# Attention behind a sorted key order, then a token mixer: longer load packets, V sorted straight onto key partitions, X turned by transposing transfers

## The chip, the cores and the metric

One core of one Trainium2 chip runs the whole program. The metric is the device time of one execution in microseconds (us): the median over runs for a kernel, the span of one profiled execution for everything that is read from the profile. Engines are named as in the profile: PE is TensorE (matmuls), PEld its weight loads, DVE VectorE, ACT ScalarE, POOL GpSimd, SP the sync engine, which here only issues transfers. Transfers (DMA) run on 16 DMA engines whoever issues them.

## The reference

q, k and v have shape 4 x 8 x 768 x 64 (batch, head, token, feature), float32. The tokens of a head form 8 blocks of 96. A small matrix P per head, made of `sort_net` by five rounds of a Sinkhorn normalization, mixes the blocks of k and v; attention then runs inside each block; its output x (4 x 768 x 512) goes through a mixer over tokens.

```python
for _ in range(5):
    P = exp(P - max(P, -1)); P = P / sum(P, -1); P = P / sum(P, -2)
k_sorted = einsum('bhij,bhjcd->bhicd', P, k_blocks)
v_sorted = einsum('bhij,bhjcd->bhicd', P, v_blocks)
attn = softmax(q_blocks @ k_sorted^T / 8)          # inside each block of 96
x = (attn @ v_sorted) as (batch, token, 512)
wq, wk = x @ w_q, x @ w_k                           # 512 -> 64
mixed = (wq @ wk^T / 8) @ x
out = relu(mixed) @ w_out
```

## The kernel before

Everything is bf16 in SBUF, with float32 sums in PSUM. The work is cut into some 30 kinds of units, each named by a letter, the batch b and a running number n: `K21` is unit 1 of the K sort of batch 2. A capital letter is TensorE work that fills one or two of the eight PSUM banks; the small letter is the copy or the arithmetic that empties them, on ACT (A) or DVE (D). All units stand in one list, `ORDER`, written out as a table; every engine runs its own units in the order of that list, and semaphores hold it to the data. Nothing is reordered at run time, so a unit that waits holds everything behind it on its engine.

For one batch the stages are:

- `l` loads q, k and v, float32 to bf16 on the way, from the POOL queue; 128 partitions hold 128 groups of 6 neighbouring tokens of a head, so that a packet is 6 x 64 elements. The first q is loaded in float32 by two transfers of the sync queue and cast by `z`.
- `a`, `c`: the Sinkhorn rounds, exponentials on ACT and sums on DVE, once for all 32 heads. `B`, `u`, `n` spread the result into the sorting matrices M (`n`: one product with a mask, 512 elements per partition and half a batch).
- `Q`/`q`: q is turned so that features lie on partitions (QT). `K`/`k`: k is sorted and turned by one matmul with M (KT); the copy also brings the tokens back into block order.
- V. In batch 0, `Y`/`y` sort it like k, and `F`/`f` turn the result back so that keys lie on partitions (VT). In batches 1 to 3, `V`/`v` multiply with M as the weight and V as the moving side (three units of 8 matmuls, 128 columns each); the result Vs still has groups of tokens on partitions, and `R`, six transfers SBUF to SBUF per batch from the sync queue, moves it onto key partitions (VT).
- `S` scores (two heads side by side in the rows of the array), `e` exponential, `P` attention weights times V with a column of ones for the sums, `r` reciprocal, `x` product into X (96 keys x 512 features per block).
- `T`/`t` turn X on TensorE (batches 0 to 2), `D` turns it by two transposing transfers of the sync queue (batch 3), into XT. `J`/`j` multiply with w_q and w_k, `d` copies the q half to other partitions, `W`/`w` turn the k half, `G`/`g` and `H`/`h` are the mixer, `O`/`o` the output product with w_out, `s` the store.
- `U`/`z` turn the weights w_q and w_k into place, since they are loaded in long rows too. `Z` are matmuls on zeros that keep TensorE busy during the Sinkhorn rounds.

After the last unit a guard reduces the reciprocals on POOL and would take a slow general path for extreme numbers; it isn't taken here.

Of the kernel before, what the change touches and what calls it, by code (L numbers as in the profile page):

```python
# [8 lines left out]
FP32 = mybir.dt.float32  # L9
# [8 lines left out]
ORDER = """
i00:G i02:D lk0 c00:D lv0 A00:5 a01:A c01:D Z09:4 a02:A:5 z10:A c02:D Q00:7 a03:A c03:D z11:G i03:G
a04:A Q01:5 Z06:6 z13:A c04:D a05:A c05:D z12:G Q03:1 Q02:0 q03:D:1 q01:A:5 B00:3 n00:D:3 K00:4  # L20
n03:D:3 q00:A:7 K03:6 u00:A:3 q02:A:0 k00:A:4 n01:D:3 n02:D:3 k03:D:6 K01:0 Y02:2 k01:A:0 lv1 K02:4
lk1 y02:A:2 n11:G Y03:6 k02:D:4 y03:A:6 Y01:0 n10:G Y00:2 S06:4 F03:6 F02:7 y00:D:2 f03:D:6 f02:D:7
e06:A:4 S01:4 y01:A:0 e01:A:4 S00:2 F01:0 F00:1 S02:4 f01:D:0 V11:6 lq1 e00:A:2 V12:2 e02:A:4
f00:D:1 v11:D:6 v12:A:2 P00:0 n20:G V10:4 S03:6 v10:A:4 P01:2 r00:D:0 x00:D:0 e03:A:6 K13:0 k13:A:0
r01:D:2 x01:D:2 lp K11:4 k11:D:4 S05:6 K12:2 K10:0 e05:A:6 S04:4 k12:D:2 R10:S T00:6 e04:A:4 Q13:7
Q11:2 t00:D:6 k10:A:0 q13:D:7 R12:S Q10:3 R11:S P02:4 q11:D:2 r02:D:4 S16:0 S12:6 q10:A:3 P03:2
R13:S e16:A:0 U00:0 x02:D:4 r03:D:2 S11:4 lq2 x03:D:2 lk2 n30:G e12:A:6 S15:6 R14:S Q12:1 R15:S
z01:A:0 n21:G q12:D:1 T01:0 t01:D:0 P04:2 e11:A:4 T02:5 r04:D:2 x04:D:2 U01:4 S14:0 lv2 e15:A:6
z02:D:4 e14:A:0 n31:G S10:6 S13:2 T03:4 t03:D:4 lq3 Q20:0 e13:A:2 Q21:1 t02:D:5 q20:D:0 P12:2 lk3
q21:D:1 r12:D:2 e10:A:6 Q22:4 Q23:0 P11:6 x12:D:2 J01:1 r11:D:6 J00:5 q22:A:4 K23:2 x11:D:6 j01:D:1  # L30
q23:A:0 K21:6 j00:A:5 k23:A:2 K22:4 K20:0 k21:D:6 S25:2 k22:A:4 P14:6 W00:4 e25:A:2 T11:5 k20:D:0
W01:4 r14:D:6 t11:A:5 S26:2 e26:A:2 P13:0 x14:D:6 d00:S r13:D:0 w00:A:4 V21:6 V20:2 V22:4 x13:D:0
v20:D:2 T12:1 t12:D:1 d01:S T13:0 v21:A:6 v22:A:4 P10:6 S24:2 S22:4 lv3 G00:1 t13:D:0 r10:D:6 G01:1
e24:A:2 S21:2 x10:D:6 e22:A:4 Q33:0 Q30:6 g00:D:1 e21:A:2 T10:1 q33:D:0 q30:D:6 R21:S S20:4 H02:2
H01:6 t10:D:1 R25:S Q31:0 J10:1 R22:S h02:A:2 q31:D:0 H00:2 Q32:0 h01:D:6 e20:A:4 h00:D:2 S23:4
j10:A:1 J11:1 K33:6 R20:S K30:2 q32:D:0 e23:A:4 K31:4 R24:S j11:A:1 K32:0 k33:A:6 k30:D:2 k32:D:0
k31:A:4 R23:S S35:6 e35:A:6 S30:2 S32:4 S36:6 P21:0 r21:D:0 e30:A:2 P23:2 e36:A:6 e32:A:4 x21:D:0
r23:D:2 V31:6 V30:0 lo v31:A:6 v30:A:0 V32:4 v32:A:4 W11:7 x23:D:2 P22:2 R34:S W10:7 O02:6 P24:0
r22:D:2 x22:D:2 w10:A:7 R33:S P20:4 T22:7 o02:A:6 t22:A:7 r24:D:0 d11:S T21:3 t21:A:3 r20:D:4 R30:S
x24:D:0 O01:6 x20:D:4 T23:7 S34:0 S33:4 S31:2 R31:S e33:A:4 t23:D:7 G10:7 d10:S G11:7 e34:A:0  # L40
o01:A:6 e31:A:2 T20:4 g10:D:7 O00:5 H10:0 H11:6 t20:D:4 h10:D:0 R32:S h11:A:6 J21:4 o00:D:5 J20:2
j21:A:4 R35:S j20:A:2 P30:6 W21:3 P31:4 W20:3 s00:S r30:D:6 x30:D:6 P32:0 O03:2 r31:D:4 w20:A:3
P34:6 O05:3 x31:D:4 d21:S r32:D:0 o03:A:2 x32:D:0 r34:D:6 o05:A:3 P33:4 d20:S G20:2 G21:2 x34:D:6
H12:6 D30:S g20:A:2 h12:A:6 r33:D:4 O10:0 x33:D:4 H20:4 H22:2 H21:6 o10:D:0 O11:1 O12:0 D31:S
h21:D:6 h20:A:4 o11:A:1 o12:D:0 O04:6 o04:D:6 O13:1 O22:0 J31:7 j31:D:7 h22:A:2 J30:2 s10:S O14:3
s01:S W31:7 o13:A:1 o22:A:0 j30:A:2 w31:A:7 W30:6 O23:1 w30:A:6 d30:D o23:A:1 o14:D:3 s11:S d31:D
G30:0 s02:S G31:0 O15:7 g30:A:0 H31:4 H32:2 H30:0 h31:D:4 O20:6 o15:A:7 O21:7 O25:4 o21:D:7 o20:A:6
h32:A:2 O24:5 s12:S O34:3 O315:6 h30:A:0 s21:S o24:A:5 O314:0 O35:1 o25:D:4 o315:A:6 o314:A:0
o34:D:3 s20:S O32:6 s22:S O31:5 s314:A s34:A O33:7 o32:A:6 o35:D:1 O30:6 s315:A s35:S o33:A:7
o30:A:6 s32:S o31:D:5 s31:S s30:A s33:S  # L50
# [4 lines left out]
def kernel(  # L55
# [63 lines left out]
    XT = tiles("XT", 2, [P, PT, S])  # L119
# [28 lines left out]

# [24 lines left out]
    def u_a(b, n, e, bank):  # L173
        nc.scalar.activation(Pv, Pv, ACT.Exp)  # L174
# [18 lines left out]


# [6 lines left out]
    def u_i(b, n, e, bank):  # L201
# [274 lines left out]

    def guard():
# [213 lines left out]
```

## Time and profile before

| | us |
|---|---|
| median of 3 runs | 106.07 (105.77 to 108.18) |
| profiled execution: span from its first to its last instruction | 103.3 |
| mean granted TensorE clock, share of full speed | 0.983 |

The profile gives no other time of its own for that execution; the median of the runs lies 2.8 us over its span. In the rows shown below, a group row names the line, the engine, the operation and its tiles (output <- inputs) with partitions x elements, then count, busy time, mean duration in ns, and the idle time before. A timeline row begins with start and time in us, then engine, line, operation, tiles, and `xN` for N instructions in a row. In the page's slices one digit stands for a fortieth of the span and gives tenths. All matmuls share one line of code, L156, and all copies two (L160 on ACT, L164 on DVE), so tiles tell them apart.

### The profile page before, as it was taken

The page shows a single profiled execution, that of the slowest core. Times are in us where ns is not written, and L with a number is a line of the kernel's source. Part 1 is how long each engine was busy: PE and PEld are TensorE (multiplying, and loading weights), DVE is VectorE, ACT ScalarE, POOL GpSimd, SP SyncE. Part 2 cuts the span into 40 slices and gives each one's busy share as a digit, 9 for nine tenths or more (in the row PEclk, how much of TensorE's full clock was granted, in tenths as well). Part 3 has the DMA queues.
Part 4 walks back from the last instruction along what each step waited for, and adds up shares of the span by engine and source line. Part 5 has one row for each costly group of instructions (what it writes and reads, how often), then busy time and mean ns, then how long its engine had stood idle before and what let it go on. Part 6 is the DMA issues. An engine that isn't in the chain of part 4 may idle for free.

```text
span 103.3 us, 3449 instructions
## 1 busy us (share of the span) xinstructions
PE 86.1 (83%) x1461; PEld 61.6 (60%) x1467; DVE 70.7 (68%) x137; ACT 71.1 (69%) x103; POOL 26.2 (25%) x43
## 2 busy tenths in 40 slices
PE   4947259998996969989899668999998999999950
PEld 2234159897784756978667457785874445546510
DVE  2677784799986797969879747957899733355210
ACT  4263667799899555897868889879646574558440
POOL 7376348690499700000000000000005700000000
PEclk9999995999999999999999999999999999999999
DMA  1799999999999999999999900264335799168993
GB/s 25 283 334 213 203 203 206 203 204 206 199 239 249 230 204 204 205 208 216 199 236 246 213 14 0 69 173 116 141 106 129 175 400 382 43 247 362 347 348 117
DMA packets 22032, 20.91 MB, mean 202 GB/s; under 512 B 4097, under 2 KB 20353, under 8 KB 22017
## 3 DMA queue, kind: packets, MB, share of 16 engines
q0 software_dynamic: 12256, 9.31, 58.1%
q1 hardware_dynamic: 9184, 10.73, 31.4%
q10 hardware_dynamic: 576, 0.66, 1.7%
q8 instruction: 11, 0.18, 0.7%
q14 instruction: 5, 0.03, 0.1%
HBM read 20.19 MB, written 6.29 MB: 256 GB/s over the span
## 4 chain that ended last, share of the span: by engine, by line
PE 33%; DMA 22%; DVE 21%; issue 8%; ACT 8%; SPq 2%; POOL 2%; ACTq 0%; DVEq 0%
PE ps L156 33%; DMA Qn<-in_q_dram 11%; DMA VT<-Vs 8%; DVE X L384 8%; ACT E L355 4%; SPq L316 2%; DVE Rall L379 2%; DMA out_dram<-ot 2%; POOL M L254 2%; DVE KT L164 2%; ACT ot L160 2%; DMA Pm<-in_sort_net_dram 1%; DVE Pm L197 1%; DVE tmp L195 1%; ACT Pm L174 1%
## 5 line engine op out<-in xcount | busy, mean ns | idle before, releaser
L355 ACT ACTIVATE E<-ps 96x960 bf16<-96x960 f32 (+1 forms) x28 | 24.0, 899 | 4.1 <-PE ps L156 3.8
L156 PE MATMUL ps<-wo,mixT 128*128 128x512 bf16 (+1 forms) x98 | 21.6, 362 | 0.4 <-issue 0.2
L384 DVE TENSOR_TENSOR X<-ps,Rall 96x896 bf16<-96x896 f32 (+1 forms) x20 | 20.0, 1003 | 0.6
L156 PEld LDWEIGHTS <-mixT 128*128 128x128 bf16 x104 | 9.5, 98 | 8.9 <-issue 0.8
L160 ACT COPY ot<-ps 128x512 f32<-128x512 f32 (+2 forms) x17 | 9.5, 560 | 6.9 <-PE ps L156 6.6
L156 PE MATMUL ps<-VT,E 96*128 96x65 bf16 x256 | 11.0, 193 | 0.9 <-DMA VT<-Vs 0.7
L487 POOL CROSS_LANE_REDUCE s<-Rall 96x1 f32<-96x280 f32 x1 | 0.8, 756 | 42.8 <-DVE Rall L379 42.8
L156 PEld LDWEIGHTS <-E 96*128 96x128 bf16 x256 | 9.5, 97 | 2.6 <-DMA VT<-Vs 0.8
L156 PEld LDWEIGHTS <-KT 64*128 64x128 bf16 (+1 forms) x288 | 8.3, 97 | 4.1 <-issue 2.6
L156 PE MATMUL ps<-QT,KT 64*128 64x96 bf16 x256 | 8.9, 204 | 2.1 <-ACT E L355 1.0
L156 PE MATMUL ps<-idb,Qn 128*64 128x128 bf16 x192 | 7.5, 222 | 3.8 <-ACT Qn L160 2.2
L164 DVE COPY ot<-ps 128x512 f32<-128x512 f32 (+1 forms) x10 | 6.4, 637 | 5.9 <-PE ps L156 4.8
L164 DVE CAST KT<-ps 128x768 bf16<-128x768 f32 x9 | 8.4, 953 | 2.8 <-PE ps L156 2.5
L254 POOL TENSOR_TENSOR M<-PTR,m_p 128x512 bf16<-128x512 bf16 x6 | 7.8, 1304 | 8.4 <-PE ps L156 5.5
L156 PEld LDWEIGHTS <-Qn 128*64 128x64 bf16 x192 | 5.7, 109 | 6.0 <-ACT Qn L160 3.2
L447 ACT ACTIVATE mixT<-ps 128x1024 bf16<-128x1024 f32 x7 | 7.1, 1025 | 3.0 <-PE ps L156 3.0
L156 PE MATMUL ps<-M,Kn 128*64 128x128 bf16 x192 | 7.5, 231 | 1.9 <-ACT QT L160 0.6
L160 ACT CAST KT<-ps 128x768 bf16<-128x768 f32 x11 | 8.6, 801 | 0.7 <-PE ps L156 0.7
L156 PEld LDWEIGHTS <-Kn 128*64 128x64 bf16 x192 | 6.6, 116 | 2.8 <-issue 1.8
L379 DVE RECIPROCAL Rall<-ps 96x14 f32<-96x14 f32 (+1 forms) x20 | 4.6, 228 | 4.8 <-PE ps L156 4.5
L449 DVE TENSOR_SCALAR mixT<-ps 128x1024 bf16<-128x1024 f32 x5 | 6.0, 1221 | 2.4 <-PE ps L156 2.3
L160 ACT CAST Vs<-ps 128x1024 bf16<-128x1024 f32 x7 | 6.8, 1019 | 0.6 <-ACT E L355 0.4
(81 smaller groups left out, 130.8 us busy)
## 6 DMA issues: line engine op xcount, KB each, us to landing
out_dram<-ot SPq DMA_DIRECT2D x9, 512.0 KB, 3.5
Kn<-in_k_dram POOLq DMA_DIRECT2D x4, 768.0 KB, 15.4
Vn<-in_v_dram POOLq DMA_DIRECT2D x4, 768.0 KB, 13.1
VT<-Vs SPq DMA_DIRECT2D x18, 132.0 KB, 6.6
Qn<-in_q_dram POOLq DMA_DIRECT2D x3, 768.0 KB, 14.0
XT<-in_q_dram SPq DMA_DIRECT2D x2, 768.0 KB, 5.9
out_dram<-ot SPq DMA_DIRECT2D x3, 256.0 KB, 2.0
wo<-in_moe_w_out_dram POOLq DMA_DIRECT2D x1, 512.0 KB, 25.5
```

What stands on the lines that cost most here:

```text
L156: nc.tensor.matmul(o, w, x, is_transpose=t, start=start, stop=stop, skip_group_check=True)
L160: nc.scalar.copy(o, i)
L164: nc.vector.tensor_copy(o, i)
L174: nc.scalar.activation(Pv, Pv, ACT.Exp)
L195: nc.vector.reduce_sum(tmp, (Pm if n == 1 else Pv).rearrange("p i j -> p j i"), axis=AX.X)
L254: ENG[e].tensor_tensor(out=M[b % 2][:, h0:h0 + hn], in0=src.unsqueeze(2).to_broadcast([P, hn, SP, NB]), in1=m_p.unsqueeze(1).unsqueeze(3). ...
L316: ENG[e].dma_start(out=VT[b % 2].rearrange("(s r) i h x -> r s i (h x)", r=R6)[n], in_=Vs[0][:, n].rearrange("p h e -> p (h e)"))
L355: nc.scalar.activation(E[b % 2][:, n, 0:2 * w * BLK].rearrange("p (t a c) -> p a t c", a=2, c=BLK), PS[0:BLK, bank:bank + 2, 0:w * BLK].re ...
L379: nc.vector.reciprocal(Rall[:, b, n, :, 0:w], avps(bank, w)[:, :, :, D])
L384: nc.vector.tensor_mul(xo.rearrange("p (a t d) -> p a t d", a=2, d=D), avps(bank, w)[:, :, :, 0:D], Rall[:, b, n, :, 0:w].unsqueeze(3).to_ ...
L447: nc.scalar.activation(o, i, ACT.Relu)
L449: nc.vector.tensor_relu(o, i)
```

## The change

Six things change together, and `ORDER` is new throughout (it has 12 units of Q and of K instead of 16, and so on).

- Loads of q and k: a partition holds 24 neighbouring tokens of a head, and four heads make 128 partitions; a packet is 24 x 64 elements (3 KB in bf16). Q and K then take three units per batch of 16 matmuls, with two halves of heads in the columns of the array, and copies of 1024 columns. The first q comes in six transfers of the sync queue (three pieces of 8 tokens, two halves of heads), and ACT casts its three pieces.
- Load of V: a partition holds one block of 96 tokens (64 partitions for a batch, two batches in one tile), in packets of 8 KB read.
- V's sort: the units `V` (four per batch, 16 matmuls each, in all four batches) take for each feature d the column `Vn[..., d]`, 96 keys, as the weight, and a matrix MV of 64 columns as the moving side. The output has keys on partitions at once; `Y`, `F`, `Vs` and the transfers `R` go.
- X of batches 1, 2 and 3 is turned by transposing transfers (`D`); only batch 0 keeps `T`.
- The weights w_q, w_k are loaded straight into place; `U` goes. The masks Lk, Lv, m_k, m_v are made at the start, mostly on POOL; M is 256 elements per partition and batch.
- `W` turns both halves of qkT (8 matmuls of 128 columns), and the copy takes one half; `H` has twice the matmuls with half the columns; the last stores of batch 3 are of whole rows of 512.

```diff
 ORDER = """
-i00:G i02:D lk0 c00:D lv0 A00:5 a01:A c01:D Z09:4 a02:A:5 z10:A c02:D Q00:7 a03:A c03:D z11:G i03:G
...
+i00:G ls0:S i02:D lk0:G A00:0 ls1:S m00:A:0 lv0:G i04:G ls2:S c00:D a01:A c01:D lq1:G i03:G a02:A
+z00:A c02:D Q00:0 z01:A lk1:G Z08:1 q00:D:0 lv1:G a03:A z02:A c03:D lp:G lo:G a04:A c04:D Z06:0
...
 """
-    NIN = 3
-    Qn, Kn, Vn = (tiles(n, NIN, [P, H, R6, D]) for n in ("Qn", "Kn", "Vn"))
+    QT4 = P // NP // NB
+    CT = BLK // QT4
+    C8 = 8
+    NC = CT // C8
+    C4 = CT // R6
+    NV = 4
+    Qn = tiles("Qn", NQ, [P, 2, CT, D])
+    Kn = tiles("Kn", NK, [P, 2, CT, D])
+    Vn = tiles("Vn", 2, [P, BLK, D])
...
-    QT = tiles("QT", 2, [P, NP, R6, P])
-    KT = tiles("KT", 2, [P, NP, S + PAD])
-    Vs = tiles("Vs", 1, [P, R6, H, DV])
-    VT = tiles("VT", 2, [BLK, NB, H, DV])
+    QT = tiles("QT", 2, [P, CT, NP, NB * QT4])
+    KT = tiles("KT", 2, [P, NPR * BLK + PAD])
+    VT = tiles("VT", 2, [BLK, 2, H, NB, DV])
...
+        elif n[0] == "v":
             b = int(n[1])
-            nc.gpsimd.dma_start(out=t[b % NIN][:, h0:h1].rearrange("p h r d -> p h (r d)"),
-                                in_=src[b, h0:h1].rearrange("h (p r) d -> p h (r d)", p=P))
+            nc.gpsimd.dma_start(out=Vn[b // 2][half(b)].rearrange("p c d -> p (c d)"),
+                                in_=v[b].rearrange("h (j c) d -> (h j) (c d)", c=BLK),
+                                max_dma_last_dim=VDESC)
...
+        else:
+            t, src = {"q": (Qn, q), "k": (Kn, k)}[n[0]]
+            b = int(n[1])
+            nc.gpsimd.dma_start(out=t[b % len(t)].rearrange("p a c d -> p a (c d)"),
+                                in_=src[b].rearrange("(a h) (j c) d -> (h j) a (c d)", a=2, c=CT))
...
     def u_Q(b, n, bank):
-        for r in range(R6):
-            for hh in range(2):
-                mm(bf(bank)[hh * D:(hh + 1) * D, r * P:(r + 1) * P],
-                   Qn[b % NIN][:, 2 * n + hh, r, :], idb, t=True)
+        for c in range(C8):
+            for a in range(2):
+                mm(bf(bank)[a * D:(a + 1) * D, c * P:(c + 1) * P], Qn[b % NQ][:, a, n * C8 + c, :], idb, t=True)
...
     def u_K(b, n, bank):
-        sort_turn(Kn, b, n, bank)
+        ps = flat(bank)
+        for c in range(C8):
+            for a in range(2):
+                mm(ps[a * D:(a + 1) * D, c * P:(c + 1) * P], Kn[b % NK][:, a, n * C8 + c, :], M[:, b, a, :])
 
     def u_k(b, n, e, bank):
-        in_blocks(KT[b % 2], n, e, bank)
+        copy(e, KT[b % 2][:, 0:NPR * BLK].rearrange("p (u q n c) -> p n u q c", q=QT4, n=NC, c=C8)[:, n],
+             flat(bank).rearrange("p (c u q) -> p u q c", c=C8, q=QT4))
...
     def u_V(b, n, bank):
         ps = flat(bank)
-        for h in range(H):
-            mm(ps[:, h * P:(h + 1) * P], M[b % 2][:, h].rearrange("p s i -> p (s i)"),
-               Vn[b % NIN][:, h, 2 * n:2 * n + 2, :].rearrange("p r d -> p (r d)"))
+        for m in range(D // NV):
+            mm(ps[0:BLK, m * D:(m + 1) * D], Vn[b // 2][half(b), :, n * D // NV + m], MV[half(b), b // 2, :])
 
     def u_v(b, n, e, bank):
-        copy(e, Vs[0][:, 2 * n:2 * n + 2, :, 0:D].rearrange("p r h d -> p h r d"),
-             flat(bank).rearrange("p (h r d) -> p h r d", h=H, r=2))
-
-    def u_R(b, n, e, bank):
-        ENG[e].dma_start(out=VT[b % 2].rearrange("(s r) i h x -> r s i (h x)", r=R6)[n],
-                         in_=Vs[0][:, n].rearrange("p h e -> p (h e)"))
...
+        w = D // NV
+        copy(e, VT[b // 2][:, b % 2].rearrange("p h i x -> p (h i) x")[:, :, n * w:(n + 1) * w],
+             flat(bank)[0:BLK, :].rearrange("p (d u) -> p u d", d=w))
 
     def u_S(b, n, bank):
...
-                   KT[b % 2][o:o + D, kp, i * BLK:i * BLK + P],
-                   QT[b % 2][o:o + D, kp, :, i * SP:(i + 1) * SP])
+                   KT[b % 2][o:o + D, pr * BLK:pr * BLK + P],
+                   QT[b % 2][o:o + D, :, kp, i * QT4:(i + 1) * QT4].rearrange("p (c r) t -> p r c t", r=R6))
...
     def u_W(b, n, bank):
+        if n >= 10:
+            for i in range(NB):
+                mm(bf(bank)[0:BLK, i * P:(i + 1) * P], qkT[b % 2][:, i * BLK:(i + 1) * BLK], idb, t=True)
+            return
...
     def u_H(b, n, bank):
         for p2 in range(2):
-            for a in range(2):
-                qq = (qkT, qD)[a][b % 2][a * DH:(a + 1) * DH, :]
-                mm(PS[:, bank + a, p2 * 256:(p2 + 1) * 256],
-                   Ab[b % 2][a * DH:(a + 1) * DH, p2 * P:(p2 + 1) * P],
-                   qq.rearrange("p (i r s) -> p r i s", i=NB, r=R6)[:, 2 * n:2 * n + 2])
+            for r in range(2):
+                for a in range(2):
+                    qq = (qkT, qD)[a][b % 2][a * DH:(a + 1) * DH, :]
+                    mm(PS[:, bank + a, p2 * 256 + r * P:p2 * 256 + (r + 1) * P],
+                       Ab[b % 2][a * DH:(a + 1) * DH, p2 * P:(p2 + 1) * P],
+                       qq.rearrange("p (i r c t) -> p r i t c", i=NB, r=R6, c=C4)[:, 2 * n + r])
```

What the change moves on three engines is shown by the order of their instructions, before and after. On the sync queue, behind the load of q of batch 0 (VT the sorted V, Vs its form before the transfers, qD and qkT the mixer's q), there stood:

```order
L316 DMA VT_86<-Vs_84 16x8x528 x6
L411 DMA qD_95<-qkT_93 64x384 x2
L316 DMA VT_85<-Vs_84 16x8x528 x6
L316 DMA VT_86<-Vs_84 16x8x528 x2
L411 DMA qD_96<-qkT_94 64x384
```

Now there stands, at the same place (XT is X turned, ot the output's buffer):

```order
L397 DMA qD_90<-qkT_88 64x384 x2
L376 DMA_TRANSPOSE XT<-X_86 128x16x96 x2
L461 DMA out_dram<-ot_100 128x1024
L397 DMA qD_91<-qkT_89 64x384 x2
L376 DMA_TRANSPOSE XT<-X_85 128x16x96 x2
```

The transfers of sorted V are gone, and transposing transfers of X stand between those of qD. On ACT, at the start of the program (Pm is the Sinkhorn matrix, Qn q of batch 0 in bf16), before:

```order
L174 ACTIVATE Pm<-Pm 32x64 x2
L176 CAST m_p<-ps 128x16
L160 CAST Qn_69<-XT_91 128x768
L174 ACTIVATE Pm<-Pm 32x64
L178 COPY Lx<-idb 32x512
```

and after:

```order
L182 ACTIVATE Pm<-Pm 32x64 x2
L168 CAST Qn_69<-XT 128x2x512 x2
L182 ACTIVATE Pm<-Pm 32x64
L168 CAST Qn_69<-XT 128x2x512
L182 ACTIVATE Pm<-Pm 32x64 x2
```

Two casts of q now stand ahead of the third exponential and one ahead of the fourth; POOL had a part of them before. On TensorE, in a unit of V's sort (M and MV the sorting matrices, Vn the loaded V), before:

```order
L156 LDWEIGHTS M_109
L156 MATMUL ps<-Vn_77,M_109 128x128
L156 LDWEIGHTS M_109
L156 MATMUL ps<-Vn_77,M_109 128x128
L156 LDWEIGHTS M_109
```

and after:

```order
L164 LDWEIGHTS Vn_74
L164 MATMUL ps<-MV,Vn_74 96x64
L164 LDWEIGHTS Vn_74
L164 MATMUL ps<-MV,Vn_74 96x64
L164 LDWEIGHTS Vn_74
```

V has moved from the moving side to the weights.

More of the change, by code (lines that the diff above doesn't have):

```diff
@@ L23 @@
[L23 to L40, printed above, removed]
@@ L449, in u_h @@
             nc.vector.tensor_relu(o, i)
[L451 to L454 removed]
     def u_O(b, n, bank):
[L457 removed]
         for t in range(PT):
[L459 to L460 removed]
+            mm(PS[:, bank, :], mixT[b % 2][:, t // 2, t % 2, n, :], wo[:, t, :], start=(t == 0), stop=(t == PT - 1))
     def oslot(b, n):
```

219 lines of the change are left out of this document (110 added, 109 removed).

## The prediction, made blind

> **What bounds the kernel now.** I read the page's header, slices and chain first, then the timeline of TensorE and the groups by shape.
>
> ```profile
> span 103.3 us, 3449 instructions
> PE 86.1 (83%) x1461; PEld 61.6 (60%) x1467; DVE 70.7 (68%) x137; ACT 71.1 (69%) x103; POOL 26.2 (25%) x43
> PE   4947259998996969989899668999998999999950
> GB/s 25 283 334 213 203 203 206 203 204 206 199 239 249 230 204 204 205 208 216 199 236 246 213 14 0 69 173 116 141 106 129 175 400 382 43 247 362 347 348 117
> q0 software_dynamic: 12256, 9.31, 58.1%
> HBM read 20.19 MB, written 6.29 MB: 256 GB/s over the span
> PE ps L156 33%; DMA Qn<-in_q_dram 11%; DMA VT<-Vs 8%; DVE X L384 8%; ACT E L355 4%; SPq L316 2%; DVE Rall L379 2%; DMA out_dram<-ot 2%; POOL M L254 2%; DVE KT L164 2%; ACT ot L160 2%; DMA Pm<-in_sort_net_dram 1%; DVE Pm L197 1%; DVE tmp L195 1%; ACT Pm L174 1%
> ```
>
> The busy shares of 68 to 83% name no bound, so I cut the program at the first sorting matmul of V of batch 3. These timeline rows of TensorE (start, time, operation) give the cut, its two ends and the rates I use; the rate is (time of the row minus one matmul's own latency) over (count minus one).
>
> ```profile
> 13.42 0.86 PE L156 MATMUL ps<-M,Kn 128*64 128x128 bf16 x24 [0.52 <-DVE M L254]
> 19.97 0.60 PE L156 MATMUL ps<-QT,KT 64*128 64x96 bf16 x20
> 20.50 1.09 PE L156 MATMUL ps<-idb,KT 128*96 128x128 bf16 x16
> 41.31 1.53 PE L156 MATMUL ps<-M,Kn 128*64 128x128 bf16 x48
> 44.94 0.61 PE L156 MATMUL ps<-VT,E 96*128 96x65 bf16 x14
> 45.39 1.50 PE L156 MATMUL ps<-Vn,M 128*128 128x128 bf16 x24
> 47.01 0.84 PE L156 MATMUL ps<-idb,X 96*128 96x96 bf16 x16
> 61.07 0.61 PE L156 MATMUL ps<-Vn,M 128*128 128x128 bf16 x8
> 68.45 1.06 PE L156 MATMUL ps<-X,wk 96*64 96x256 bf16 x16
> 71.30 1.47 PE L156 MATMUL ps<-XT,wqk 128*128 128x384 bf16 x8
> 80.17 4.49 PE L156 MATMUL ps<-wo,mixT 128*128 128x512 bf16 x20
> 86.66 0.51 PE L156 MATMUL ps<-idb,qkT 128*96 128x64 bf16 x8
> 90.69 8.83 PE L156 MATMUL ps<-wo,mixT 128*128 128x512 bf16 x47
> ```
>
> ```profile
> L156 PE MATMUL ps<-Vn,M x72: 216/219/229, 21.8 to 63.1; 128*128 128x128 bf16 x72
> ```
>
> With that latency of 0.2 us (0.3 to 0.4 for the rows of 384 and 512 columns) this makes 28 ns for a matmul of K or a turn of q, some 20 for a score, 32 for E times V, 56 for V's sort, 58 for a turn of sorted V, 42 for a turn of X, 43 for a turn of wk, 52 for G, 163 for XT, 216 for the output. The order puts into stage A (13.4 to 61.1, 47.7 us) 240 matmuls of K and of V's f32 sort and 144 turns of q (10.8 us), 226 scores (4.5), 156 of E times V (5.0), 48 sorts and 32 turns of V (4.6), 64 turns of X (2.7), 16 XT (2.6) and small ones (2.3): 32.4 us, 68%. Stage B (61.1 to 99.5, 38.4 us) holds the equal of 96 output matmuls (20.7), 100 of E times V (3.2), 16 XT (2.6), 48 G (2.5) and 6.3 of the rest: 35.3 us, 92%. So stage B is bound by TensorE, and stage A by something else: loads, copies and VT's transfer, which the chain names. Behind the last matmul come 3.8 us of copy and store up to 103.3, and 106.07 (the median) lies 2.8 us over the span of the profiled execution. I add 6.6 us to the end of TensorE's work.
>
> **The change part by part.** *Loads.* 203 to 206 GB/s stand in the load slices, and queue 0 counts written bf16 bytes (9.31 MB against 20.19 MB read), so the read rate is near 406 GB/s, as fast as the store slices at their best (400). Longer packets I cost at nothing: from no gain up to 2 us if 5% were left. VT's SBUF transfers go, 12 of them inside the load phase; the transposing transfers of batch 1 come in.
>
> ```profile
> VT<-Vs SPq DMA_DIRECT2D x18, 132.0 KB, 6.6
> XT<-X SPq DMA_TRANSPOSE x2, 3.7
> wo<-in_moe_w_out_dram POOLq DMA_DIRECT2D x1, 512.0 KB, 25.5
> 34.74 0.78 POOL L228 DMA_DIRECT2D wo<-in_moe_w_out_dram x1
> ```
>
> The last load lands at 34.7 + 25.5 = 60.2. Twelve transfers are 1.6 MB, 4 us at 400 GB/s and 8 at 203; I take 5. The two transposing ones cost 0 (hidden) to 7.4 (two landings); I take 2. The last load, now V of batch 3, then lands near 57. That is a floor for the cut, no gain by itself.
>
> On the sync queue the six VT transfers of a batch and their waits are replaced by two of X (the first pair of orders above). Nothing waits at E times V for a transfer any more; what waits for the transposing one is J, several units behind.
>
> *Copies.* The rows by shape:
>
> ```profile
> L160 ACT CAST KT<-ps 128x768 bf16<-128x768 f32 x11 | 8.6, 801 | 0.7 <-PE ps L156 0.7
> L164 DVE CAST KT<-ps 128x768 bf16<-128x768 f32 x9 | 8.4, 953 | 2.8 <-PE ps L156 2.5 <-ACT KT L160 0.2
> L160 ACT CAST Vs<-ps 128x1024 bf16<-128x1024 f32 x7 | 6.8, 1019 | 0.6 <-ACT E L355 0.4
> L164 DVE COPY QT<-ps 128x768 bf16<-128x768 bf16 x10 | 5.3, 548 | 1.9 <-PE ps L156 1.9
> L164 DVE COPY XT<-ps 128x768 bf16<-128x768 bf16 x9 | 4.8, 552 | 1.0 <-PE ps L156 0.7
> L164 DVE COPY VT<-ps 96x1024 bf16<-96x1024 bf16 x4 | 2.6, 680 | 0.2 <-PE ps L156 0.2
> L164 DVE CAST Vs<-ps 128x1024 bf16<-128x1024 f32 x2 | 2.4, 1217 | 0.0
> ```
>
> Twelve copies of turned X become 4; K goes from 16 of 768 to 12 of 1024 columns; V's 9 + 4 (Vs and the f32 sort of batch 0) + 4 (VT) become 16 of 1024; q's 16 become 12. At these durations (1024 columns of q by VT's 680 on DVE, 1.0 on ACT) DVE saves 4.9 us and ACT 3.3 in all. Because the order moves seven exponentials behind the cut, stage A itself loses 6.9 us of DVE and 5.2 of ACT. KT was read from PSUM with large steps already, so the stepped reads of the new copies cost nothing extra.
>
> *Start.* ACT now casts q in three pieces of 1024 columns (0.83 us x 1024/768 = 1.1) between the exponentials of the Sinkhorn chain (the second pair).
>
> ```profile
> 6.85 0.26 ACT L174 ACTIVATE Pm<-Pm 32x64 f32<-32x64 f32 x1
> 8.61 0.26 ACT L174 ACTIVATE Pm<-Pm 32x64 f32<-32x64 f32 x1 [1.00 <-DVE Pm L197]
> 8.79 0.83 ACT L160 CAST Qn<-XT 128x768 bf16<-128x768 f32 x1
> ```
>
> Pieces of q thus stand ahead of the exponentials that ran at 6.85 and 8.61, and the last q landed only for 8.79. Waiting for it and casting (8.8 + 1.1 = 9.9) puts the fourth exponential 1.3 us later; with a q copy that DVE now has inside the chain I take 1.5 (bounds 0.5 and 3). K starts at 14.9.
>
> *V's weights, the term that decides.* In the third pair of orders the data became the weight: 96 columns that lie 64 elements (128 bytes) apart, with 64 moving columns. There are 256 such pairs for 72 of 56 ns, 48 of 28 and 32 of 58 (7.2 us). The lower bound is the turn of wk, also 96 weight columns against 64 moving ones but side by side: 43 ns. No weight of this trace is read with steps. The nearest rows are a reduction on DVE over the same 32x64 tile, along rows (L190) and across them with 32-byte steps (L195):
>
> ```profile
> L190 DVE TENSOR_REDUCE tmp<-Pm x5: 207/207/207, 3.1 to 10.8; 32x8 f32<-32x64 f32 x5
> L195 DVE TENSOR_REDUCE tmp<-Pm x5: 253/255/269, 3.8 to 11.5; 32x8 f32<-32x64 f32 x4, 32x8 f32<-32x72 f32 x1
> ```
>
> Eight more stepped elements cost 14 ns, 1.75 ns each; KT and Vs casts of DVE give (1217 - 953)/256 = 1.03 ns for one more element elsewhere. Stepped reading is 1.7 times as slow. Taken as a ratio, a pair costs 43 x 1.7 = 73 ns; taken as a time, 96 x 1.75 = 168. I take 73, as an engine's own rate scales with it, and keep 43 and 168 as ends.
>
> [...]
>
> *TensorE's sum.* In stage A the order now holds 304 matmuls of K and turns of q (8.5 us), 178 scores (3.6), 142 of E times V (4.5), 32 turns of X (1.3), 12 XT (2.0), 12 output matmuls (2.6) and 2.0 of small ones: 24.5 us, and 192 of V's pairs. Stage B: 84 output matmuls (18.1), 114 of E times V (3.6), 20 XT (3.3), 48 G (2.5), 78 scores (1.6) and 4.3 of the rest: 33.4 us, and 64 pairs. At 73 ns that is 38.5 and 38.1 (before 32.4 and 35.3). For stage A's filling I take 80%, midway between 68% (copies and loads, which are relieved) and 92% (TensorE alone): 38.5/0.80 = 48.1. So the cut falls at 14.9 + 48.1 = 63.0, TensorE ends 38.1/0.92 = 41.4 later at 104.4, and with 6.6 the time is 111.0. Stage A at 92% is held by the loads to 57 and gives 105.0; at 68% it gives 119.5. H's matmuls of 128 columns in twice the number, and turns of wk with 128 columns, I cost at 0.4 us, within these.
>
> **The rivals.** *Steps cost the weights nothing* (43 ns). Stage A holds 32.7 us of TensorE work and is bound by copies: 47.7 - 5.2 (ACT, the smaller gain) = 42.5, cut at 57.4, just over the loads; stage B 36.2/0.92 = 39.3; 103.3 us. For it: 128 weight columns of E are loaded every 32 ns and 96 of wk's turn only every 43, so the path that reads weights has slack in one of them. Against: the reduction rows. Range 101 to 106.
>
> *A line costs a fixed time* (168 ns): TensorE binds both stages at 92%: 56.8/0.92 = 61.7, 44.2/0.92 = 48.0, 131.2 us. For it: 1.75 ns is the only direct reading. Against: it is a reading of another engine, which takes 1.03 ns for an element side by side where a weight column takes 43/96 = 0.45.
>
> *The transposing transfers come late.* They queue among the loads; if batch 1's land only when loads end (57 + 3.7), J and with it the cut in the fixed order stand at 61, as before, even with free weights: 61 + 39.3 + 6.6 = 106.9. For it speak VT's transfers, which took 6.6 us to land among the loads; against it J's distance of some ten units from the issue.
>
> **How the numbers follow.** Forecast 0.43, free steps 0.37, fixed line time 0.12, late transfers 0.08. A measurement of this kernel tells about 2% from no change: 103.9 to 108.2. Faster: four fifths of the free case, 0.30. Same: the rest of it, most of the late case and a quarter near the lower end of the forecast, 0.20. Slower: 0.50. The forecast's own range is 105 to 119.5; with the free case the range for 8 in 10 is 101 to 119.5, leaving out the fixed line time. The time is that of the likeliest, 111.0.
>
> **What would show it.** The spacing of the 16 matmuls in a unit of V: about 0.7 us a unit is the free case, 1.2 to 1.4 the forecast, 2.7 the fixed time. The fourth exponential near 9.9 and the first K near 14.9 show the start right. The first V unit of batch 3 near 63 with TensorE above 75% before it shows stage A; near 57 the free case. J of batch 1 waiting for a transfer shows the late case; the last load landing near 57 shows the loads' sum. The forecast is wrong if V's units run at 0.7 us and the cut falls before 60.

## The result: 152.1 us, where 111.0 was forecast

The changed kernel takes 152.14 us (median of 6 runs, 150.63 to 152.99) against 105.85 (104.51 to 108.18, 6 runs): a ratio of 1.4385 with a 95% interval of 1.4283 to 1.4488. The direction was forecast, the size was not: 152 lies far outside 101 to 119.5. Some runs of the experiments had a lower clock than others of the same kernel; ratios, and the times of e1, e3 and e9 below, leave them out.

The page of the changed kernel: header, slices of TensorE and its clock, first queue, chain by line, and the two costliest groups (busy us, mean ns of one, idle time before). Behind it stands the clock's slices of the kernel before.

```profile
span 148.8 us, 3565 instructions
PE 128.5 (86%) x1542; PEld 101.0 (68%) x1542; DVE 67.9 (46%) x121; ACT 70.2 (47%) x93; POOL 21.6 (15%) x52
PE   1392039999999999999899999999999999999980
PEclk9999555555589555557975599999975799999998
q0 software_dynamic: 4368, 9.31, 33.4%
PE ps L164 76%; DMA XT<-in_q_dram 9%; DVE X L370 1%; SPq L256 1%; ACT KT L168 1%; ACT E L341 1%; ACT Qn L168 1%; ACT QT L168 1%; ACT ot L168 0%; DVE tmp L202 0%; DVE Rall L365 0%; DVE Pm L201 0%; DVE tmp L199 0%; ACT Pm L182 0%; DVE tmp L203 0%
L164 PE MATMUL ps<-MV,Vn 64*96 64x64 bf16 x256 | 43.4, 339 | 0.0
L164 PEld LDWEIGHTS <-Vn 64*96 64x96 bf16 x256 | 42.6, 253 | 0.4 <-issue 0.2
```

```profile
PEclk9999995999999999999999999999999999999999
```

Three things differ from the page of before. The chain is three quarters TensorE, where it was one third; the costliest group is V's sort, 43.4 us busy where all of V's sort and turns came to 7.2 by the forecast's rates; and TensorE's slices are full or nearly so from the seventh to the last but one, although its clock stands at half speed in 15 of the 40 slices (mean 0.778, before 0.983). DVE and ACT have hardly less work (67.9 and 70.2 us, before 70.7 and 71.1) but wait for it: the view of waits puts 27.7 us of DVE's and 19.2 of ACT's idle time down to copies of V that wait for TensorE.

The timeline of TensorE shows the start (first two rows), a turn of X beside a unit of V, and the first unit of V of batch 3:

```profile
23.84 2.77 PE L164 MATMUL ps<-M,Kn 128*64 128x128 bf16 x48
26.54 9.69 PE L164 MATMUL ps<-MV,Vn 64*96 64x64 bf16 x58
54.81 2.10 PE L164 MATMUL ps<-idb,X 96*128 96x96 bf16 x24
56.84 2.82 PE L164 MATMUL ps<-MV,Vn 64*96 64x64 bf16 x16
95.60 2.77 PE L164 MATMUL ps<-MV,Vn 64*96 64x64 bf16 x16
```

The first K stands at 23.84, where 13.42 was before and 14.9 was forecast. A unit of V takes 2.6 us from start to start (16 pairs of 163 ns, the median distance of two starts). The X row gives (2.10 - 0.28)/23 = 79 ns a turn, by the reading of the forecast that made it 42 before: the granted clock is 0.50 from 54 to 57 us, where it was 1.00 at the turns of before (47.0 to 47.8). The cut of the forecast, the first unit of V of batch 3, is at 95.6 instead of 63.

ACT's timeline shows why K is late:

```profile
4.94 1.03 ACT L168 CAST Qn<-XT 128x1024 bf16<-128x1024 f32 x1
11.68 1.04 ACT L168 CAST Qn<-XT 128x1024 bf16<-128x1024 f32 x1 [5.71 <-DMA XT<-in_q_dram]
12.63 0.25 ACT L182 ACTIVATE Pm<-Pm 32x64 f32<-32x64 f32 x1
17.47 1.04 ACT L168 CAST Qn<-XT 128x1024 bf16<-128x1024 f32 x1 [4.59 <-DMA XT<-in_q_dram]
18.42 0.25 ACT L182 ACTIVATE Pm<-Pm 32x64 f32<-32x64 f32 x1
```

The second and the third piece of q land for 11.68 and 17.47, and the third and fourth exponential of the Sinkhorn chain, which stand behind their casts in ACT's row, run at 12.63 and 18.42 (before 6.85 and 8.61). So there are two suspects, the steps of V's weights and the late q, and a third that may only follow from them, the halved clock.

### The profile page after: what moved, and what is told of

It is laid out like the page before. It is cut to its first block, busy times and chain, and to the rows that moved or that the text cites. A ratio compares the mean times of both kernels' runs of the same rounds, so it can differ in the third digit from the quotient of the medians.

```text
span 148.8 us, 3565 instructions
## 1 busy us (share of the span) xinstructions
PE 128.5 (86%) x1542; PEld 101.0 (68%) x1542; DVE 67.9 (46%) x121; ACT 70.2 (47%) x93; POOL 21.6 (15%) x52
## 4 chain that ended last, share of the span: by engine, by line
PE 76%; DMA 9%; ACT 5%; DVE 4%; SPq 2%; issue 1%; ACTq 0%; DVEq 0%
PE ps L164 76%; DMA XT<-in_q_dram 9%; DVE X L370 1%; SPq L256 1%; ACT KT L168 1%; ACT E L341 1%; ACT Qn L168 1%; ACT QT L168 1%; ACT ot L168 0%; DVE tmp L202 0%; DVE Rall L365 0%; DVE Pm L201 0%; DVE tmp L199 0%; ACT Pm L182 0%; DVE tmp L203 0%
## 5 line engine op out<-in xcount | busy, mean ns | idle before, releaser
L164 PE MATMUL ps<-MV,Vn 64*96 64x64 bf16 x256 | 43.4, 339 | 0.0
L164 PEld LDWEIGHTS <-Vn 64*96 64x96 bf16 x256 | 42.6, 253 | 0.4 <-issue 0.2
L164 PE MATMUL ps<-wo,mixT 128*128 128x512 bf16 x96 | 24.7, 400 | 0.0
L172 DVE CAST VT<-ps 96x1024 bf16<-96x1024 f32 x9 | 11.0, 1221 | 27.7 <-PE ps L164 27.7
L168 ACT CAST VT<-ps 96x1024 bf16<-96x1024 f32 x7 | 7.1, 1015 | 19.2 <-PE ps L164 19.2
L168 ACT COPY ot<-ps 128x512 f32<-128x512 f32 x15 | 8.7, 587 | 8.1 <-PE ps L164 7.0
L164 PEld LDWEIGHTS <-KT 64*128 64x128 bf16 x256 | 9.8, 111 | 3.5 <-issue 2.4
L168 ACT CAST KT<-ps 128x1024 bf16<-128x1024 f32 x10 | 9.8, 1015 | 2.7 <-PE ps L164 2.6
L172 DVE COPY ot<-ps 128x512 f32<-128x512 f32 x9 | 6.2, 687 | 5.8 <-PE ps L164 5.7
L172 DVE COPY QT<-ps 128x1024 bf16<-128x1024 bf16 x9 | 6.2, 685 | 4.7 <-PE ps L164 4.6
```

Source lines behind the costliest of these rows:

```text
L164: nc.tensor.matmul(o, w, x, is_transpose=t, start=start, stop=stop, skip_group_check=True)
L168: nc.scalar.copy(o, i)
L172: nc.vector.tensor_copy(o, i)
```

## The experiments

They are called e1 to e10 in the order in which they were run. Times are medians, with a ratio to runs of the kernel before on the same chip where there were several rounds. e5, an earlier form of e10, gave no time. Of longer edits the lines that matter are shown; `...` marks what is left out.

**e1: the steps of the weights taken away.** In this kernel and the others with weights side by side, V's weights are read from the same tile in another order, so the output is of other data; the number of pairs, the matmul shapes and the loads stay.

```diff
+VSTEP = (1, 1, 1, 1)
...
-mm(ps[0:BLK, m * D:(m + 1) * D], Vn[b // 2][half(b), :, n * D // NV + m], MV[half(b), b // 2, :])
+st = VSTEP[b]
+w = Vn[b // 2][half(b)].rearrange("p c d -> p (c d)")
+o = (n * D // NV + m) * (BLK if st == 1 else 1)
+mm(ps[0:BLK, m * D:(m + 1) * D], w[:, o:o + (BLK - 1) * st + 1:st], MV[half(b), b // 2, :])
```

> The changed kernel, with V's weights read side by side (96 neighbouring elements of the same tile instead of one feature of 96 keys; V's sort and so the output are of other data, everything else is the same work). Theory S (a weight column that lies 128 bytes from its neighbour costs a fixed 1.7 ns, so a pair took 163 ns): the pairs come down to 43 to 46 ns, TensorE loses 256 x 0.119 = 30 us of work, mean granted clock back above 0.9, time 112 to 120, since the late start (K at 23.8 instead of 13.4) stays. Rival C (the halved clock is the cause and V its victim): pairs stay above 80 ns, clock stays below 0.85, time above 140.

Measured: 115.0 us, a ratio of 1.0833 (1.0723 to 1.0944). A row of its timeline and the groups of its waits at TensorE:

```profile
44.55 0.90 PE L165 MATMUL ps<-MV,Vn 64*96 64x64 bf16 x16
PE ps L165 <- ACT Qn L169: 12.6, 2, 8.4
```

A pair takes 45 ns. 256 x (163 - 45) = 30.2 us of the 37 us gained are the pairs themselves; the rest comes with a clock whose mean rises from 0.778 to 0.935, and this run doesn't take it apart. The steps are shown to be the main cause. Some 9 us over the kernel before are left, and the waits name the casts of q.

**e4 and e8: what a step costs.** Two kernels gave each batch another step in V's weights (output of other data but where the step is 64): the code of e1 with steps of 2, 4, 8 and 16 elements in the first, and of 1, 4, 2 and 64 in the second:

```diff
+VSTEP = (2, 4, 8, 16)
```

> The changed kernel with another step between V's weight columns in each batch: 2, 4, 8 and 16 elements (4, 8, 16, 32 bytes) for batches 0 to 3 (V's sort of other data). If the price goes by 16-byte lines at 1.7 ns each: 43 ns a pair at step 2 (4 columns a line), about 82 at step 4, 163 at 8 and at 16. [...] If any step costs the full price: 163 at all four.

> The weights of V in steps of 1, 4, 2 and 64 elements of 2 bytes for the batches 0, 1, 2 and 3 (output of other data for batches 0 to 2). In e4 the step of 2 elements fell into a stretch in which the granted clock was 0.50, where e3 shows 80 ns a pair for weights side by side too. Theory S (a load of weights takes a time for each 16 bytes touched by its reading, some 1.7 to 1.9 ns, so for 96 columns 24 x 1.8 = 43 ns with 2 elements' steps, which hides behind the pair's own 45): batch 1 near 91 ns a pair, batch 2 near 45 (80 where the clock is 0.50), batch 3 at 163. Rival (any step but 1 costs a price of its own, or the price goes with the clock): batch 2 at 80 with the clock at 1.00, or batch 1 and 3 other than 91 and 163. Time by S near 126: 116.7, 64 x 46 ns for batch 1 and 64 x 118 ns for batch 3 more, and a lower clock in batch 3.

Measured: 143.06 and 128.43 us, one run each. Units of V in the timelines, first two of the first kernel (steps of 8 and 16 elements), then three of the second (4, 2 and 64):

```profile
78.41 2.96 PE L165 MATMUL ps<-MV,Vn 64*96 64x64 bf16 x16
85.91 3.02 PE L165 MATMUL ps<-MV,Vn 64*96 64x64 bf16 x16
```

```profile
46.94 1.65 PE L165 MATMUL ps<-MV,Vn 64*96 64x64 bf16 x16
60.97 2.40 PE L165 MATMUL ps<-MV,Vn 64*96 64x64 bf16 x48
73.02 2.77 PE L165 MATMUL ps<-MV,Vn 64*96 64x64 bf16 x16
```

The median distances of two starts, with the clock granted in the unit's stretch (the row of 2 bytes from e1, e3 and e8, that of 128 bytes from the changed kernel and e8, the others from e4 and e8):

| step of the 96 columns | at clock 1.00 | at clock 0.50 |
|---|---|---|
| 2 bytes (side by side) | 45 ns | 80 ns |
| 4 bytes | 47 ns | 80 ns |
| 8 bytes | 91 ns | 91 ns |
| 16 bytes | 176 ns | 176 ns |
| 32 bytes | 180 ns | 180 ns |
| 128 bytes | 163 ns | 163 ns |

Up to 4 bytes the pair is as fast as side by side and goes with the clock. From 8 bytes on it doesn't go with the clock; at 1.00 it about doubles from 4 to 8 and from 8 to 16 bytes (47, 91, 176 ns) and grows no further (180, 163). So I count by the 16-byte pieces that the 96 columns touch (48 at 8 bytes, 96 from 16 bytes on): 91/48 to 163/96, 1.7 to 1.9 ns a piece everywhere; at 4 bytes the same count makes 24 x 1.85 = 44 ns, an estimate that lies within the 45 of a pair side by side. The expectation by this count (91, 45, 163) came out. Two columns in a piece (8 bytes' steps) cost 91 ns against 45 side by side, and four (4 bytes' steps) 47.

**e2, e3, e6 and e7: the late q.** The packets by start time, from the transfer records of the trace (number of packets in 1 us, mean ns of one):

```
          before: queue 0 | queue 1    after: queue 0 | queue 1
 4-5 us      0            252, 65         51, 249       67, 70
 5-6 us      0            276, 61         49, 250       50, 95
 6-7 us     81, 78        170, 70         48, 247       48, 96
 8-9 us    252, 78         23, 51         49, 254       49, 94
12-13 us   268, 79          0             39, 322       42, 96
```

Queue 0 carries GpSimd's loads, queue 1 the sync queue's q (16 of its 67 packets from 4 to 5 us are of 4 bytes only). Before, q had the transfers to itself up to 6 us, and 387 and 399 GB/s in the two rows from 4 us on. Now k0, issued at 1.52 us (before at 1.45), sends from 4.1 us on where it was 6.2, and the two queues are served packet by packet: 48 of one, 48 of the other. A packet of k0 is 3072 bytes written, one of q 2048, so q gets two fifths, about 100 GB/s.

A first edit held k0 and v0 back until the second piece of q had landed, by a copy on GpSimd that reads its last element, once on the changed kernel (e2) and once together with weights side by side (e3):

```diff
-i00:G ls0:S i02:D lk0:G A00:0 ls1:S m00:A:0 lv0:G i04:G ls2:S c00:D a01:A c01:D lq1:G i03:G a02:A
-z00:A c02:D Q00:0 z01:A lk1:G Z08:1 q00:D:0 lv1:G a03:A z02:A c03:D lp:G lo:G a04:A c04:D Z06:0
+i00:G ls0:S i02:D A00:0 ls1:S m00:A:0 i04:G ls2:S c00:D a01:A c01:D i03:G a02:A
+z00:A c02:D Q00:0 y01:G lk0:G lv0:G lq1:G lk1:G z01:A Z08:1 q00:D:0 lv1:G a03:A z02:A c03:D lp:G lo:G a04:A c04:D Z06:0
...
+def u_y(b, n, e, bank):
+    nc.gpsimd.tensor_copy(gate, q32[:, 1, (n + 1) * C8 - 1, D - 1:D])
```

> The changed kernel, with the first k and v loads (and those behind them on the POOL queue) issued only when the second of the three pieces of the first q has landed. Theory L (long load packets take turns one for one with q's 2 KB packets, so q gets a third of the bandwidth and holds the Sinkhorn chain on ACT): the last piece of q lands near 7 to 8 instead of 17, the first K matmul near 14 instead of 23.8, time 140 to 145. Rival I (the six issues of the sync queue, up to 4.1 us, or the casts themselves hold it): q still lands after 12, time above 148.

> Both edits together (V's sort of other data, as in the first). If the two causes are all that is wrong, the time is that of the case 'steps cost nothing' of the prediction: 102 to 106. If something else in the new layout or order costs (transposing transfers, H's new reading order, the order itself), 108 or more; then the profile shows where.

e2 takes 152.38 us (ratio 1.4366, 1.4259 to 1.4473): nothing is gained, theory L's time is missed, and the time is that of rival I although its reason is not there, since the last cast of q starts at 8.57. e3 takes 115.9, no better than e1 and not 102 to 106. TensorE's timeline of e2 and GpSimd's of e3 (in brackets the time idle before, and what ended it):

```profile
15.03 1.53 PE L165 MATMUL ps<-M,Kn 128*64 128x128 bf16 x48
28.05 4.15 PE L165 MATMUL ps<-MV,Vn 64*96 64x64 bf16 x25 [11.49 <-POOL MV L288]
```

```profile
14.07 0.61 POOL L244 DMA_DIRECT2D wqk<-in_moe_w_k_dram  x1 [1.47 <-DMA Kn<-in_k_dram]
18.00 0.61 POOL L248 DMA_DIRECT2D wo<-in_moe_w_out_dram  x1 [3.31 <-DMA Vn<-in_v_dram]
22.34 0.61 POOL L248 DMA_DIRECT2D wo<-in_moe_w_out_dram  x1 [3.73 <-DMA Qn<-in_q_dram]
26.31 0.71 POOL L263 DMA_DIRECT2D Qn<-in_q_dram  x1 [3.36 <-DMA Kn<-in_k_dram]
27.03 1.26 POOL L289 TENSOR_TENSOR MV<-ot,m_v 64x64 bf16<-64x64 bf16 x4
```

K did start 9 us earlier, at 15.03. But in e3 the ninth load on GpSimd's queue was issued only when the first (k0) had landed, the tenth behind v0, the eleventh behind q1, the twelfth behind k1. So no more than eight were under way, and MV, the moving side of V's sort, is made by the same engine behind them. The wait had only moved.

The next edit, on the code of e2 and e3, put the products MV and M ahead of the loads of wo and q2, with the steps of the weights (e7) and with weights side by side (e6):

```diff
-z00:A c02:D Q00:0 y01:G lk0:G lv0:G lq1:G lk1:G z01:A Z08:1 q00:D:0 lv1:G a03:A z02:A c03:D lp:G lo:G a04:A c04:D Z06:0
+z00:A c02:D Q00:0 y01:G lk0:G lv0:G lq1:G lk1:G z01:A Z08:1 q00:D:0 lv1:G a03:A z02:A c03:D lp:G a04:A c04:D Z06:0
-a05:A c05:D Q02:0 q02:A:0 B00:1 Q01:2 u00:A:1 n00:D:1 B01:3 q01:D:2 lq2:G K02:0 u01:A:3 K01:4
+a05:A c05:D Q02:0 q02:A:0 B00:1 Q01:2 u00:A:1 n00:D:1 B01:3 q01:D:2 K02:0 u01:A:3 K01:4
-N00:G k02:A:0 K00:2 k01:D:4 N01:G V02:6 k00:A:2 n01:G V00:0 v02:D:6 n02:G V01:4 v00:A:0 V03:2
-lk2:G v01:D:4 S06:6 S01:0 lv2:G e06:A:6 e01:A:0 S04:6 n03:G v03:D:2 S02:4 e04:A:6 Q10:0 e02:A:4
+N00:G k02:A:0 K00:2 k01:D:4 N01:G V02:6 k00:A:2 n01:G V00:0 v02:D:6 n02:G n03:G lq2:G V01:4 v00:A:0 V03:2
+lk2:G v01:D:4 S06:6 S01:0 lv2:G e06:A:6 e01:A:0 S04:6 lo:G v03:D:2 S02:4 e04:A:6 Q10:0 e02:A:4
```

> The same two edits of the start on the kernel after itself: the weights of V at their steps of 128 bytes, the whole computation. Theory Q: the first V unit comes 9 to 10 us sooner and the rest is TensorE's 256 pairs of 163 ns, which are on the path all through, so the time falls by 7 to 10: 142 to 146. Rival R: 149 to 153 as in e2, the start's gain is eaten again by a later wait.

> The weights of V side by side (the output is then of other data, as in e1), the loads of k0 and v0 held back until the second piece of q has landed, as in e3, and GpSimd's row mended: in e3 the ninth to twelfth load on GpSimd's queue were issued only when the first to fourth had landed (a load of wo waited 3.3 us for v0 and 3.7 for q1, the one of q2 3.4 for k1), and the four products MV of GpSimd stood behind them, so TensorE waited 11.0 us for MV. Here the products MV and M stand ahead of the loads of wo and q2. Theory Q (with the weights' price away, what is left of e1's 10.5 us over the kernel before is the start and this queue alone): the wait for MV goes, the first V unit starts near 17.5 instead of 27.4, and the time is 104 to 109. Rival R (something else of the change costs it: the order, the strided moving reads, the transposing transfers, the loads' floor): 112 to 117, with TensorE's waits elsewhere.

Measured: e7, the whole computation with the mended start, takes 142.28 us (ratio 1.348, 1.3341 to 1.3619), 9.9 less than the changed kernel, inside what was expected. e6 takes 110.37 (ratio 1.0458, 1.0353 to 1.0562), between the two theories. The timeline of TensorE and the clock of e6:

```profile
14.81 1.53 PE L166 MATMUL ps<-M,Kn 128*64 128x128 bf16 x48
17.83 0.86 PE L166 MATMUL ps<-MV,Vn 64*96 64x64 bf16 x15 [1.50 <-POOL M L279]
PEclk9999999556999999997559999999999999999999
```

K stands at 14.81 and V at 17.83, ten us earlier than in e1, of which 4.6 arrive at the end. The edits of e6 together take away 41.8 of the 46.3 us; the clock, granted at 0.50 in two stretches (19 to 26 and 50 to 57 us), is the next suspect for the rest.

**e10: is it the length of the packets?** The changed kernel with shorter packets for k0 and v0 alone, 768 bytes written as before:

```diff
+if n == "k0":
+    for a in range(2):
+        nc.gpsimd.dma_start(out=t[0][:, a].rearrange("p c d -> p (c d)"),
+                            in_=src[0, a * (H // 2):(a + 1) * (H // 2)].rearrange("h (j c) d -> (h j) (c d)", c=CT),
+                            max_dma_last_dim=1536)
+    return
...
-                                max_dma_last_dim=VDESC)
+                                max_dma_last_dim=1536 if b == 0 else VDESC)
```

> The kernel after, with one thing changed: the loads of k0 (in two transfers) and v0 read 6 tokens (768 bytes written) in a packet, as before, not 24 or 32 (3072 and 4096 bytes written). Theory P (from 4 us on the packets of the software queue and of the hardware queue were passed on about one to one, so the queue with the shorter packets gets the smaller share): q gets about 2048 of 2816 parts of the rate, some 180 GB/s where it had 100, its third piece is converted near 11 to 12 us instead of 17.5, and the first K matmul comes near 17 instead of 23.8. Rival T (it is the earlier arrival of k0's packets, 4.0 us where it was 6.2, and their length doesn't matter): the third conversion stays at 17 to 18 and K at 23 to 24. The time falls less than the start, 143 to 150 by P, 150 to 153 by T.

```profile
10.54 1.04 ACT L168 CAST Qn<-XT 128x1024 bf16<-128x1024 f32 x1 [4.56 <-DMA XT<-in_q_dram]
14.09 1.04 ACT L168 CAST Qn<-XT 128x1024 bf16<-128x1024 f32 x1 [2.35 <-DMA XT<-in_q_dram]
20.46 2.77 PE L164 MATMUL ps<-M,Kn 128*64 128x128 bf16 x48
28.93 3.31 PE L164 MATMUL ps<-MV,Vn 64*96 64x64 bf16 x20 [5.70 <-POOL MV L293]
```

These rows of ACT and TensorE answer half way. The third cast of q is at 14.09, between 11 to 12 (length alone) and 17 to 18 (length without influence), and K 3.4 us earlier. From 8 to 11 us q had 172 to 207 GB/s at about as many packets of the one queue as of the other, as expected; but from 4 to 6 us queue 0 had 144 and 134 packets against 52 and 51, which one-to-one service doesn't explain. So the length of the packets is shown to be one cause; why queue 0 was served more often in those first 2 us stays open. k0's packets came from 4.0 us on here too, and no run puts them back to 6.2 us with the packets long, so that their earlier arrival is a second cause is not shown. One run took 156.36 us, more than the changed kernel: k0 is two loads here, one more on GpSimd's queue, and MV came late, so that TensorE waited 5.7 us for it.

**e9: the clock.** The kernel of e6 and 20 matmuls on zeros, unread, in the places where TensorE waits (parts of three rows of `ORDER`):

```diff
-a05:A c05:D Q02:0 q02:A:0 B00:1
+a05:A c05:D Q02:0 Z07:3 q02:A:0 B00:1
...
-N01:G V02:6 k00:A:2
+N01:G Z07:7 V02:6 k00:A:2
...
-q20:D:2 P10:0 k21:A:6 G01:3
+q20:D:2 P10:0 k21:A:6 Z06:5 G01:3
```

> e6 (weights side by side, output of other data; loads of k0 and v0 held back; GpSimd's row mended) with 20 more matmuls on zeros whose results nobody reads, in the three places where e6's TensorE waits: 7 behind the turns Q02 (1.7 us of waiting for PbT), 7 ahead of the first V unit (1.5 us), 6 ahead of the second G unit of batch 0 (1.4 and 0.5 us). In e6 the granted clock is 0.50 in two stretches, 19.x to 26 and 50 to 57 us, each behind some 3 to 6 us in which TensorE was busy for 35 to 65%; 1 - 0.936 of its 108.2 us is 6.9 us of lost clock, against 1.7 us in the kernel before. Theory C (the 5 us by which e6 is longer than before are this lost clock): with the waits filled the clock stays near 1.00 there, the mean is 0.96 to 0.98, and the time is 105 to 108. Rival D (the clock falls for another reason, or the time hangs on other waits): the two stretches at 0.50 stay, and the time is 109.5 to 112.5, longer by what the fillers push back.

Measured: 107.98 and 109.17 us, a ratio of 1.0271 (1.0166 to 1.0377), at clocks of 0.992 and 0.982. Two stretches of e6 and the same of e9 in the windows' columns (stretch, its length, busy PE with count, clock, DMA share, GB/s):

```profile
21.00:23.00 2.00, 1.82 (x35) 0.50 1.11 218
52.00:54.00 2.00, 2.00 (x36) 0.50 1.11 193
```

```profile
21.00:23.00 2.00, 1.63 (x52) 1.00 1.11 220
52.00:54.00 2.00, 2.00 (x52) 1.00 1.05 211
```

The fillers keep the clock up in both places, so the falls there do go with TensorE's waits. But they win only 1 to 2 us of the 5: they push the first K to 15.65, and in the profiled execution (109.92 us) the clock falls in a stretch elsewhere (units of V at 80 ns from 36.6 to 40.6). The two times have the clock back, at 0.992 and 0.982, and are still some 3 us over the kernel before: lost clock alone is not the rest. K comes 2.2 us later than in the kernel before, which would be most of these 3 us; that was read from the traces and not tried.

No version here beats the kernel before. One that computes the right output with weights side by side would need V with its features outermost; what it costs to bring V into that layout was not tried.

## Why the prediction was wrong

*V's weights: the steps were named, their size taken from the wrong reading.* The step that failed is "I take 73, as an engine's own rate scales with it". The longest of the reductions, a single instruction, gave 1.75 ns for a stepped element, a time; I turned it into a ratio of 1.7 and applied that to TensorE's faster rate (43 ns for 96 columns). The runs show a time: 163/96 = 1.70 ns a column, which doesn't even follow TensorE's clock. The rival with a fixed time of 1.75 ns for each of the 96 stepped columns (168 ns; it calls one a line) was the right one and had 0.12. The argument against it, that it is another engine's reading, was the weak one. Why 1.75 and 1.70 lie so close no run shows; at steps of 16 and 32 bytes a column took 1.83 and 1.88. The miss in the pairs is 256 x (163 - 73) = 23.0 us.

*Even the right rival gave 131.2.* The missing 21 us are three sums. K started at 23.84, not 14.9: 8.9. Stage A took 71.8 us, not 61.7, and what lies behind the cut 56.5 (to the median), not 54.6: 10.1 and 1.9. The windows of stage A and of stage B up to 140 us say why (as above, with the weight loads, DVE, ACT and POOL between PE and the clock):

```profile
23.84:95.60 71.76, 70.44 (x924) 62.66 (x921) 33.89 (x46) 35.33 (x41) 7.19 (x13) 0.66 0.53 94
95.60:140.00 44.40, 44.21 (x524) 31.30 (x518) 24.39 (x36) 25.00 (x35) 3.24 (x7) 0.92 0.51 138
```

TensorE is busy for 98% of stage A at a mean clock of 0.66. Without the 192 pairs (31.3 us) 39.1 us are left for work that the sum put at 24.5 at full clock, and 24.5/0.66 = 37.1. A busy time counts each matmul's whole recorded length (one of V's stands at 339 ns on the page, though they follow each other at 163), so it is no like measure: in the kernel before stage A was busy for 41.6 us at a clock of 0.96, where the sum had 32.4:

```profile
13.42:61.07 47.65, 41.59 (x974) 34.88 (x974) 37.60 (x60) 39.33 (x52) 15.79 (x16) 0.96 1.24 208
```

Weighted by the clock record of the trace, the 39.1 us are 27.4 us at full clock, so 11.7 us are lost clock, about the 10.1 that stage A was longer than the rival's sum. No term of mine had a clock in it; I had read 0.983 off the page of before and carried it over.

*The start: the chain was right, its one assumption wrong.* "Waiting for it and casting (8.8 + 1.1 = 9.9)" took q's arrival as fixed at 8.8, and "longer packets I cost at nothing" looked at the rate of the loads alone, not at who shares it. The third piece was there only for the cast at 17.47. With q first, the fourth exponential stands at 9.73 and the first K at 14.81 in e6, against 9.9 and 14.9 forecast.

*The loads.* The last packet of the loads ends at 60.1, not 57, since GpSimd's row, which issues them, waited 16.4 us for TensorE; in e6 it ends at 56.4. The floor was about right, and no cut reached it.

*Copies.* DVE and ACT save 2.8 and 0.9 us in all, not 4.9 and 3.3. It made no difference, as both wait for TensorE.

*Transposing transfers.* J waits for none of them in any trace, so the late rival fell. The 2 us that they were to cost the loads can't be told apart in these runs.

*Stage B and the free case.* With pairs at 45 ns and the start mended, e6 takes 46.2 us behind the cut, where the free case had 39.3 + 6.6 = 45.9. That sum holds. That of its stage A doesn't, as the window of e6 shows:

```profile
14.80:64.19 49.39, 43.93 (x918) 37.14 (x920) 33.59 (x46) 34.78 (x41) 8.30 (x15) 0.86 1.04 187
```

Stage A takes 49.4 us, not 42.5, and the cut is at 64.2, not 57.4. TensorE's busy time is little above that of before (43.9 us, where it was 41.6), but its clock is 0.86 there, where it was 0.96; the free case had stage A bound by copies at the old clock. So in this order free steps would not have made the kernel faster either (110.4, not 103.3), and 0.30 for faster was too much.

## What to carry to other kernels

The price of the stepped weights could here be bounded before they were built: 96 pieces of 16 bytes touched, times the 1.75 ns that a stepped element took in DVE's row, make 168 ns a pair, and 163 were measured. Keep such a reading a time, and don't scale it by the engine's own rate: here 1.75 ns from a DVE row stood against 1.7 to 1.9 on TensorE, and 73 ns a pair by scaling against 163. When packets get longer, look at what shares the transfers with them in that microsecond (q had 387 and 399 GB/s alone and about 100 beside k0), and when a load is moved on an engine's queue, at every product behind it there (TensorE waited 11.49 us for MV in e2). And a sum for a saturated TensorE needs the clock that the new stretches will be granted (0.66 in stage A here), not the mean of the old page (0.983).

## What the hardware showed that was not expected

- A pair whose 96 weight columns lie 16 to 128 bytes apart took 163 to 180 ns from start to start, at granted clocks of 1.00 and 0.50 alike; at 4 bytes it took 47 and 80, nearly as side by side (45 and 80).
- The granted clock fell to 0.50 also while TensorE was recorded as always busy. In the changed kernel a row of units of V begins at 46.6 us under a clock of 1.00; the windows behind it:

```profile
45.00:48.00 3.00, 2.80 (x52) 2.53 (x47) 2.58 (x4) 2.50 (x3) 2.10 (x3) 1.00 0.35 24
48.00:51.00 3.00, 3.00 (x20) 3.00 (x20) 0.00 (x0) 1.02 (x1) 0.00 (x0) 0.61 0.96 181
51.00:54.00 3.00, 3.00 (x51) 2.77 (x52) 1.80 (x3) 1.06 (x2) 0.00 (x0) 0.50 1.08 212
```

  From 48 to 51 us there are twenty matmuls, each behind its own load of weights, with PE busy for 3.00 us and the clock at 0.61. In the profiles of the changed kernel, e2, e7 and e10, 13 of the 14 falls to 0.50 between 30 us and the last microseconds come while a unit of V runs, though such units hold only about a fifth of the time at a clock of 1.00. With weights side by side the falls behind the first K are fewer (one in e1, two in e6), but they too begin in a unit of V, so the steps alone are not shown to be their cause. What in such a unit the falls go with was not tried by itself.
- No more than eight loads of GpSimd's queue were under way at once in this program; the ninth was issued when the first had landed (in e3 at 14.07 us, 1.47 us of waiting for k0; in the changed kernel the tenth at 15.06, 4.18 us for v0). Whether the chip or the program's semaphores set that number stays open.
- The first transposing transfer of X in e6 kept the sync queue for 5.85 us, from 47.38 on, where the median of the six is 1.56, and landed 12.0 us after its start; nobody waited for it.
